# Attention of a fused attention and two-layer network kernel in blocks of 64 keys: one transpose takes two blocks, and the values of a pair go to two PSUM banks

## The chip, the cores and the metric

The kernel runs on one core of a Trainium2 chip. The metric is device time of one launch in microseconds (us). Three runs of the kernel before gave 847.7, 848.0 and 848.58; their median is 848.0.

## The reference

```
scores = q @ k.T / sqrt(64)                    # 4 batches, 8 heads, 576 tokens, 64 wide
heads 0-3: query t sees keys t-31 .. t         # local
heads 4-7: query t sees keys t, t-32, t-64, .. # strided
attn = softmax(scores);  x = attn @ v          # 2304 tokens x 512
g = s * relu(x @ w_in)**2 + b;  y = g @ w_out  # 512 -> 2048 -> 512
h = y @ w2_in;  out = (h * cos(h)) @ w2_out
```

## The kernel before, in words

The two layers take most of the time: 128x512 (or 128x384) fp32r matmuls whose operands are split into a high and a low part, so that each product is three matmuls. They are called big matmuls below. Attention is cut into 20 pairs of heads, five for each batch: two of local heads ("loc"), two of strided heads ("str", queries and keys sorted by token modulo 32, so that a residue is a block of 18 by 18) and one with what the blocks left over of all four ("rem"). Pairs are numbered from 0, so pair 10 is the first of batch 2. `j` is the head of a pair; its 64 channels lie on partitions 64j to 64j+63.

For each pair (class `Item`, one for each head): scores into one PSUM bank for each head (`pair_scores`, tile `s_ps`, L616); maximum, and before it the mask, on VectorE (`mask_max`; for batches 0 and 1 the mask is instead added by a matmul with the identity, L611); exponentials on ScalarE, one instruction for each block with its row sums (`exps`, L548); division by the sums on VectorE (`norm`, L561 to L563); transposes of the blocks on TensorE into `t_ps` (L573); a move out of PSUM on ScalarE (`tevac`, L581); the value matmuls into `o_ps` (L651); and a split of `o_ps` into `xhi` on ScalarE (L143) and `xlo` on VectorE (L146). A loc head has four 128x96 score blocks, each of two groups of 64 queries that see 96 keys; a str head has four of 126x126 (7 residues); a rem head one of 128x96 and two of 72x72.

Two stages run attention. Until batch 0 is done, pairs follow each other alone, with `FILL` dummy bf16 matmuls of 384 columns after the scores of pairs 1 to 5, and with weights of the first layer converted on VectorE between them. Then `attention()` is called between the big matmuls of the first layer's slots, and `Attention.micro` takes one step at a call: values of the pair two back, scores of the newest, then transposes of the one between. Each engine runs its list in the order in which the recording layer put it there; that order is fixed when the program is built, and the layer reorders what `micro` asks for by its own estimate. PSUM has eight banks: four tagged `acc`, three `att`, one `h`. In the second stage scores, transposes and values take turns on the three `att` banks. The probabilities of a head, and what the transposes gave, lie in six buffers (`NPB`).

Masks are made on GpSimd (POOL) at the start (L878 to L888). The loads of batch 0 (`FIRST`) stand in one list on the SP queue.

Of the kernel before, what the change touches and what calls it, by code (L numbers as in the profile page):

```python
# [20 lines left out]
P = 128  # L21
# [7 lines left out]
LG, LK = 64, 96  # L29
SG = 7 * NJ  # L30
SR = S - 4 * SG
# [19 lines left out]
NPB = 6  # L51
# [19 lines left out]
PRE = 3  # L71
WARM = 13
FILL = {1: 6, 2: 5, 3: 5, 4: 5, 5: 5}
# [37 lines left out]
def net(ctx, tc, qkl, qks, rqk, vloc, vstr, rv, wi1, wo1, wp1, wo2, wp2, s, b, out):  # L111
# [22 lines left out]
    mloc = const.tile([P, 4, LK], BF16, name="mloc")  # L134
    mstr = const.tile([SG, SG], BF16, name="mstr")
# [302 lines left out]
    def load_qk(bb, hp):  # L438
        if bb == 0 and hp >= 2:
            t = part[0][hp - 2][:, : QKW * 2].rearrange("p (t c) -> p t c", t=2)  # L440
        else:
            t = io_p.tile([P, 2, QKW], F32, tag="io", name="qk")
        src, w = (qkl, QKW) if hp < 2 else (qks, 4 * SG)
        nc.sync.dma_start(out=t[:, :, :w], in_=src[bb, hp % 2])
        qk_t[bb, hp] = t

    def load_v(bb, hp):
        if bb == 0 and hp >= 2:
            o = (hp - 2) * 4 * P
            v = part[1][0][:, o : o + 4 * P].rearrange("p (n d) -> p n d", d=P)  # L450
        else:
            v = io_p.tile([P, 8, P], F32, tag="v", name="v")
        if hp < 2:
            nc.sync.dma_start(out=v[0:LK], in_=vloc[bb, hp])
        else:
            nc.sync.dma_start(out=v[0:SG, 0:4, :], in_=vstr[bb, hp - 2])
        v_t[bb, hp] = v

    def load_rem_qk(bb):
        r = rem_p.tile([P, 4 * (LK + SR)], F32, tag="rq", name="rq")  # L460
        nc.sync.dma_start(out=r, in_=rqk[bb])
        rem_t[bb] = [
            r[:, : 4 * LK].rearrange("p (h t c) -> p h t c", h=2, t=2),
            r[:, 4 * LK :].rearrange("p (h t c) -> p h t c", h=2, t=2),
        ]

    def load_rem_v(bb):
        t = rem_p.tile([LK, 4, P], F32, tag="rv", name="rv")
# [5 lines left out]
    class Item:  # L474


        def __init__(self, bb, hp, j, kind):
            self.bb, self.hp, self.j, self.kind = bb, hp, j, kind
            self.ready = self.moved = self.stored = False
            if kind == "loc":  # L480
                self.parts = [(P, LK, 4, 0, mloc)]
            elif kind == "str":
                self.parts = [(SG, SG, 4, 0, mstr.unsqueeze(1).to_broadcast([SG, 4, SG]))]
            else:
                self.parts = [
                    (P, LK, 1, 0, mloc[:, 1:2, :]),
                    (SR, SR, 2, LK, mstr[:SR, :SR].unsqueeze(1).to_broadcast([SR, 2, SR])),
                ]
            self.tcols = []
            o = 0  # L490
            for m, k, n, _, _ in self.parts:
                self.tcols.append(o)
                o += m * n

        def score_mms(self):

            r = slice(self.j * D, (self.j + 1) * D)
            if self.kind == "rem":
                rq = rem_t[self.bb][0]
                yield 0, [(LG * hp, 0, rq[r, hp, 0, 0:LG], rq[r, hp, 1, :]) for hp in range(2)]  # L500
                res = []
                for hp in range(2):
                    rs = rem_t[self.bb][1]
                    res.append((0, LK + hp * SR, rs[r, hp, 0, :], rs[r, hp, 1, :]))
                yield 1, res
                return
            t = qk_t[self.bb, self.hp]
            res = []
            for i in range(4):
                if self.kind == "loc":  # L510
                    for g in range(2):
                        o = (2 * i + g) * LG
                        res.append((g * LG, i * LK, t[r, 0, o : o + LG], t[r, 1, o : o + LK]))
                else:
                    o = i * SG
                    res.append((0, i * SG, t[r, 0, o : o + SG], t[r, 1, o : o + SG]))
            yield 0, res

        def view(self, t, i):
            m, k, n, c, _ = self.parts[i]  # L520
            return t[:m, c : c + n * k].rearrange("p (n k) -> p n k", k=k)

        def mask_max(self, alloc):
            self.p = alloc()
            self.sm = sm_p.tile([P, 3, 4], F32, tag="sm", name="sm")
            for i, (m, k, n, c, mask) in enumerate(self.parts):
                src = self.view(self.s_ps, i)
                if not self.pe_mask:
                    dst = self.view(self.p, i)
                    nc.vector.tensor_tensor(dst, src, mask, ALU.add)  # L530
                    src = dst
                nc.vector.tensor_reduce(self.sm[:m, 0, i : i + n], src, axis=AX.X, op=ALU.max, negate=True)  # L532
                nc.vector.tensor_scalar(self.sm[:m, 0, i : i + n], self.sm[:m, 0, i : i + n], SCALE, None, ALU.mult)

        def run_transp(self, tag, alloc):
            self.moved = False
            self.transp(tag)
            yield
            with tc.high_priority():
                self.tevac(alloc, nc.scalar)  # L540
            self.moved = True

        def exps(self):
            for i, (m, k, n, c, _) in enumerate(self.parts):
                dst = self.view(self.p, i)
                src = self.view(self.s_ps, i) if self.pe_mask else dst
                for t in range(n):
                    nc.scalar.activation(  # L548
                        dst[:, t, :],
                        src[:, t, :],  # L550
                        AF.Exp,
                        bias=self.sm[:m, 0, i + t : i + t + 1],
                        scale=SCALE,
                        accum_out=self.sm[:m, 1, i + t : i + t + 1],
                    )

        def norm(self):
            for i, (m, k, n, c, _) in enumerate(self.parts):
                dst = self.view(self.p, i)
                sm = self.sm[:m, :, i : i + n]  # L560
                nc.vector.tensor_scalar_add(sm[:, 1, :], sm[:, 1, :], 1e-9)  # L561
                nc.vector.reciprocal(sm[:, 2, :], sm[:, 1, :])
                normed[0] = nc.vector.tensor_tensor(  # L563
                    dst, dst, sm[:, 2, :].unsqueeze(2).to_broadcast([m, n, k]), ALU.mult
                )

        def transp(self, tag):
            self.t_ps = psum(tag, "t_ps")
            for i, (m, k, n, c, _) in enumerate(self.parts):
                src = self.view(self.p, i)  # L570
                for t in range(n):
                    o = self.tcols[i] + t * m
                    self.moves = nc.tensor.transpose(self.t_ps[:k, o : o + m], src[:, t, :], ident[:m, :m])  # L573

        def tevac(self, alloc, eng):
            self.pt = alloc()
            for i, (m, k, n, c, _) in enumerate(self.parts):
                o = self.tcols[i]
                dst, src = self.pt[:k, o : o + n * m], self.t_ps[:k, o : o + n * m]
                if eng is nc.scalar:  # L580
                    nc.scalar.activation(dst, src, AF.Copy)  # L581
                else:
                    eng.tensor_copy(dst, src)

        def pv_mms(self, o):

            dst = o[self.j * D : (self.j + 1) * D]
            dc = slice(self.j * D, (self.j + 1) * D)
            if self.kind == "rem":
                vr = rem_t[self.bb][2]  # L590
                res = []
                for hp in range(4):
                    m, k, c = (LG, LK, hp * LG) if hp < 2 else (SR, SR, P + (hp - 2) * SR)
                    res.append((dst[:, c : c + m], vr[:k, hp, dc], self.pt[:k, c : c + m]))
                return res
            v = v_t[self.bb, self.hp]
            m, k, n = (LG, LK, 8) if self.kind == "loc" else (SG, SG, 4)
            return [
                (dst[:, i * m : (i + 1) * m], v[:k, i, dc], self.pt[:k, i * m : (i + 1) * m]) for i in range(n)
            ]  # L600

    def pair_scores(pair, tag, pe_mask):

        for it in pair:
            it.s_ps = psum(tag, "s_ps")
            it.pe_mask = pe_mask
        for parts in zip(*[it.score_mms() for it in pair]):
            if pe_mask:
                for it, (pi, _) in zip(pair, parts):
                    m, _, _, _, mask = it.parts[pi]  # L610
                    nc.tensor.matmul(  # L611
# [926 lines left out]
```

## Time and profile before

| what | value |
|---|---|
| median of three runs | 848.0 us |
| span of the profiled execution (the page gives no other time of it) | 845.1 us |
| runs less span | 2.9 us |
| PE busy, share of the span | 835.9 us, 99% |
| DVE busy | 620.4 us, 73% |
| ACT busy | 560.5 us, 66% |
| granted TensorE clock | 1.000 |

A busy PE is one with a matmul between its start and its modelled end; matmuls overlap in that sense, so the time that an instruction costs is read from its start to the start of the next one. "PEld" are the weight loads. An fp32 matmul shows as two matmuls and two weight loads, so 16 in the program are x32 in a row. A form such as "64*126 64x126" names the weights (64 partitions, 126 columns) and then the moving operand.

### The profile page before, as it was taken

What the parts mean: (1) busy time and instruction counts of PE and PEld (TensorE: products, weight loads), DVE (VectorE), ACT (ScalarE), POOL (GpSimd) and SP (SyncE); (2) the same over time, 40 slices, a digit from 0 to 9 for tenths busy, and PEclk for the clock granted to TensorE, in tenths of its full rate; (3) what the DMA queues carried; (4) which work ended last, traced back from release to release, by engine and by line L of the source; (5) the groups of instructions that cost most, each with busy time, mean ns of one, the idle gap of its engine ahead of it and who ended that gap; (6) DMA issues with size and microseconds to landing.
All of it is one profiled execution on the core that took longest, in us unless ns stands there. A gap on an engine that the chain in (4) does not pass through costs nothing.

```text
span 845.1 us, 13962 instructions
## 1 busy us (share of the span) xinstructions
PE 835.9 (99%) x5023; PEld 730.9 (86%) x5023; DVE 620.4 (73%) x1248; ACT 560.5 (66%) x1164; POOL 4.0 (0%) x15
## 2 busy tenths in 40 slices
PE   9999999999999999999999999999999999999998
PEld 6677788889888999999998988988989989889886
DVE  6999988798888779997975896664665555644553
ACT  6898978577777776876776665554754554645543
POOL 1000000000000000000000000000000000000000
PEclk9999999999999999999999999999999999999999
DMA  9855352687788997986899988655755655745412
GB/s 279 266 184 175 117 156 62 207 276 213 253 304 305 342 335 248 291 296 234 304 329 297 296 276 249 216 172 175 254 201 184 211 169 184 278 163 202 158 50 76
DMA packets 73445, 189.90 MB, mean 225 GB/s; under 512 B 7344, under 2 KB 26160, under 8 KB 73376
## 3 DMA queue, kind: packets, MB, share of 16 engines
q1 hardware_dynamic: 72080, 182.58, 65.1%
q10 hardware_dynamic: 1296, 6.42, 2.0%
q8 instruction: 40, 0.66, 0.3%
q14 instruction: 29, 0.24, 0.1%
HBM read 146.51 MB, written 42.47 MB: 224 GB/s over the span
## 4 chain that ended last, share of the span: by engine, by line
PE 88%; DVE 5%; ACT 3%; DMA 2%; issue 1%; POOL 0%; POOLq 0%; DVEq 0%; ACTq 0%
PE acc L1316 21%; PE pa L1422 14%; PE pb L1422 14%; PE acc L790 12%; PE h_ps L790 11%; PE acc L1326 11%; PE o_ps L651 2%; PE t_ps L573 1%; PE s_ps L616 1%; DMA w2s<-ow 1%; DVE xlo L146 1%; DMA wfb<-xlo 1%; ACT part L548 1%; DVE sm L532 0%; DVE gl L146 0%
## 5 line engine op out<-in xcount | busy, mean ns | idle before, releaser
L1316 PE MATMUL acc<-w2l,gh 128*128 128x512 f32 x576 | 177.9, 390 | 0.0
L1422 PE MATMUL pa<-xhi,wfl 128*128 128x384 f32 x464 | 138.2, 338 | 1.5 <-DVE h L1403 1.5
L1422 PE MATMUL pb<-xhi,wfl 128*128 128x384 f32 x464 | 137.9, 337 | 0.0
L1316 PEld LDWEIGHTS acc<-w2l,gh 128*128 128x128 f32 x576 | 107.8, 188 | 21.5
L1316 PE MATMUL acc<-w2l,gl 128*128 128x512 f32 x288 | 112.5, 391 | 0.0
L1232 ACT ACTIVATE r<-h 128x768 f32<-128x768 f32 (+1 forms) x50 | 40.8, 817 | 94.9 <-DVE h L1403 94.6
L146 DVE TENSOR_TENSOR gl<-r,gh 128x768 fp32r<-128x768 f32 (+3 forms) x90 | 71.5, 796 | 42.2 <-ACT gh L1232 39.0
L790 PE MATMUL h_ps<-xhi,w 128*128 128x512 f32 (+1 forms) x320 | 99.7, 375 | 1.4 <-ACT r L813 1.0
L790 PE MATMUL acc<-gh,w 128*128 128x512 f32 (+1 forms) x320 | 98.8, 373 | 0.4 <-ACT gh L143 0.4
L1422 PEld LDWEIGHTS pa<-xhi,wfl 128*128 128x128 f32 x464 | 85.5, 188 | 5.5 <-DVE h L1403 2.5
L1422 PEld LDWEIGHTS pb<-xhi,wfl 128*128 128x128 f32 x464 | 85.5, 188 | 3.1 <-ACT q L1433 0.4
L1326 PE MATMUL acc<-gh,w2l 128*128 128x512 f32 (+1 forms) x384 | 85.2, 336 | 0.0
L1422 PE MATMUL pa<-xlo,wfl 128*128 128x384 f32 x232 | 77.8, 335 | 0.0
L1422 PE MATMUL pb<-xlo,wfl 128*128 128x384 f32 x232 | 77.8, 335 | 0.0
L1403 DVE TENSOR_TENSOR h<-pb,q 128x384 f32<-128x384 f32 x72 | 39.9, 554 | 49.1 <-PE pb L1422 45.2
L790 PEld LDWEIGHTS h_ps<-xhi,w 128*128 128x128 f32 x320 | 58.6, 189 | 12.9 <-ACT r L813 2.2
L790 PEld LDWEIGHTS acc<-gh,w 128*128 128x128 f32 x320 | 58.3, 189 | 11.3 <-ACT gh L143 0.8
L1326 PEld LDWEIGHTS acc<-gh,w2l 128*128 128x128 f32 x384 | 59.8, 188 | 7.2
L1403 DVE TENSOR_TENSOR h<-pa,q 128x384 f32<-128x384 f32 x72 | 39.9, 554 | 33.2 <-PE pa L1422 32.5
L1316 PEld LDWEIGHTS acc<-w2l,gl 128*128 128x128 f32 x288 | 54.0, 188 | 11.3
L1263 ACT ACTIVATE r<-r 128x768 f32<-128x768 f32 (+1 forms) x50 | 40.9, 820 | 33.0 <-DVE r L1261 33.0
L1265 DVE TENSOR_TENSOR r<-h,r 128x768 f32<-128x768 f32 (+1 forms) x50 | 46.1, 925 | 18.8 <-ACT r L1263 18.4
(148 smaller groups left out, 1569.1 us busy)
## 6 DMA issues: line engine op xcount, KB each, us to landing
wfl<-wfb SPq DMA_DIRECT2D x68, 512.0 KB, 4.9
w2l<-w2s SPq DMA_DIRECT2D x60, 512.0 KB, 3.5
wfl<-wfa SPq DMA_DIRECT2D x34, 512.0 KB, 4.2
praw<-in_wp_dram SPq DMA_DIRECT2D x22, 512.0 KB, 4.9
oraw<-in_wo_dram SPq DMA_DIRECT2D x22, 512.0 KB, 4.6
wfb<-ob SPq DMA_DIRECT2D x21, 512.0 KB, 4.2
w2s<-ow SPq DMA_DIRECT2D x20, 512.0 KB, 4.2
wfl<-wfc SPq DMA_DIRECT2D x34, 256.0 KB, 4.7
```

Of the source, the lines that this page charges most:

```text
L146: return nc.vector.tensor_tensor(dst_lo, src, hi.bitcast(F32), ALU.subtract)
L548: nc.scalar.activation(dst[:, t, :], src[:, t, :], AF.Exp, bias=self.sm[:m, 0, i + t : i + t + 1], scale=SCALE, accum_out=self.sm[:m, 1, i ...
L573: self.moves = nc.tensor.transpose(self.t_ps[:k, o : o + m], src[:, t, :], ident[:m, :m])
L651: tail[0] = nc.tensor.matmul(dst, vs, pt, start=True, stop=True)
L790: nc.tensor.matmul(*args, **kw)
L1232: return nc.scalar.activation(*args, **kw)
L1263: nc.scalar.activation(r, r, AF.Sin, scale=-TWO_PI)
L1265: nc.vector.tensor_tensor(r, h[:, a:b], r, ALU.mult)
L1316: nc.tensor.matmul(accs[e], g[:, e * P : (e + 1) * P], w[:, wi, :], start=start and i == 0, stop=stop and i == 2, skip_group_check=True,)
L1326: nc.tensor.matmul(o, w[:, wi, e * P : (e + 1) * P], g[:, c : c + o.shape[1]], start=start and i == 0 and (c == 0 or e % 2 == 0), stop=sto ...
L1403: added[u] = nc.vector.tensor_tensor(hs[f][:, HALVES[half]], bank, qs[q], ALU.add)
L1422: nc.tensor.matmul(pb[bi], a, b[:, m, :], start=st and m == 0 and i == 0, stop=m == 1 and i == 2, skip_group_check=True)
```

## The change

All blocks are 64 keys wide. A loc head has groups of 32 queries (`LG` 64 to 32), four to a 128-row block, each with its 64 keys. A str block has three residues (54 rows and keys, computed 64 wide), two to a 128-row block, so that `SG` is 54 and not 126; 24 of the 32 residues are in the str pairs, and the rem pair takes eight (144 tokens) where it took four. Each head now has four 128x64 blocks in every pair (class `Pair`, in place of two `Item`). One transpose takes two blocks (128x128), a pair's four transposes fill one bank, and one 128x512 move takes all of it. After it the keys of one block lie on partitions 0 to 63 and of the other on 64 to 127, so the value matmuls use 64 rows and 64 columns of the array each, and the two row halves write two banks, `o[0]` and `o[1]`, each split to `xhi` and `xlo` apart. In the second stage a step takes the transposes of a pair, the scores of the next, and then the values of the same pair. `NPB` goes from 6 to 4, and the fill is of 256 columns with counts that keep the columns nearly the same. The values of the rem pair move to another buffer; v and rem loads grow, q and k of str pairs shrink.

```
-    def transp(self, tag):                      # per head: one per block
-            for t in range(n):
-                self.moves = nc.tensor.transpose(self.t_ps[:k, o : o + m], src[:, t, :], ident[:m, :m])
+        def transp(self, j, tag):
+            if j == 0:
+                self.t_ps = psum(tag, "t_ps")
+            for u in range(2):
+                src = self.p[:, j, 2 * u : 2 * u + 2, :].rearrange("p n k -> p (n k)")
+                o = 256 * j + P * u
+                self.moves = nc.tensor.transpose(self.t_ps[:, o : o + P], src, ident)
+        def run_move(self, alloc):
+            with tc.high_priority():
+                self.pt = alloc()
+                nc.scalar.activation(self.pt, self.t_ps, AF.Copy)
+        def scores(self, tag, pe_mask, alloc):
+            s_ps = [psum(tag, "s_ps") for _ in range(2)]
...
+            for part, po, lq, lk in self.score_mms():    # loc: 4 parts x 4 groups, str: 4 x 2
+                for j in range(2):
+                    r = slice(j * D, (j + 1) * D)
+                    self.last = nc.tensor.matmul(
+                        self.s[j][po : po + lq.shape[1], part, :], lq[r], lk[r], start=not pe_mask, stop=True, ...
+        def values(self, o):
+            for b_, c, slot_, q, w in self.value_mms():  # b_ alternates 0, 1; w = 32 (loc), 54 (str)
+                r = slice(KT * b_, KT * b_ + KT)
+                for j in range(2):
+                    d = slice(j * D, (j + 1) * D)
+                    tail[0] = nc.tensor.matmul(
+                        o[b_][d, c : c + w], v[r, slot_, d], self.pt[r, 256 * j + q : 256 * j + q + w], start=True, stop=True
+                    )
+        def dests(self, o):                      # two halves, each its own xhi and xlo
...
 def micro(self):
-                if done:
-                    while not (done[0].moved and done[1].moved):
-                        tick()
-                    spawn(run_values(*done, self.tags[2]))
...
+                    while self.valued < q - 1:
+                        self.values()
+                        yield
+                    if old:
+                        yield from self.transposes(old)
+                    if new:
+                        with tc.issue_after(tail[0].ins):
+                            self.scores(new, q)
+                    yield
+                    self.values()
+                    yield
...
-    for g in range(2):
-        m = mloc[g * LG : (g + 1) * LG]
+    for a in range(4):
+        m = mloc[a * LG : (a + 1) * LG]
         for base, km, cm in ((-1, 1, -1), (32, -1, 1)):
             nc.gpsimd.affine_select(
-                out=m, in_=m, ..., pattern=[[0, 4], [km, LK]], channel_multiplier=cm
+                out=m, in_=m, ..., pattern=[[0, 4], [km, KT]], channel_multiplier=cm
...
+    nc.gpsimd.memset(mrem[:, 1:4, :], NEG)       # then 6 memsets and 12 selects of 64x54
...
-NPB = 6
+NPB = 4
-FILL = {1: 6, 2: 5, 3: 5, 4: 5, 5: 5}
+FILL = {1: 9, 2: 8, 3: 8, 4: 8, 5: 8}
```

On PE before, around the values of pair 10 (bank `o_ps_1824`), the last transposes of the pair, twelve big matmuls, and then the values in one run:

```order
L573 MATMUL t_ps_1797<-ident_87,part21_102 96x128 x4
L790 MATMUL h_ps_1802<-xhi_92,w0_345 128x512
L790 MATMUL h_ps_1802<-xlo_93,w0_345 128x512
L790 MATMUL h_ps_1802<-xhi_92,w0_345 128x512 x2
L790 MATMUL h_ps_1802<-xlo_93,w0_345 128x512
L790 MATMUL h_ps_1802<-xhi_92,w0_345 128x512 x2
L790 MATMUL h_ps_1802<-xlo_93,w0_345 128x512
L790 MATMUL h_ps_1802<-xhi_92,w0_345 128x512 x2
L790 MATMUL h_ps_1802<-xlo_93,w0_345 128x512
L790 MATMUL h_ps_1802<-xhi_92,w0_345 128x512
L651 MATMUL o_ps_1824<-part21_102,v_1616 64x64 x16
L616 MATMUL s_ps_1841<-qk_1716 126x126
```

On PE now, the end of the 32 score matmuls of pair 11 (`s_ps_1496`, `s_ps_1497`), which stand right behind the last transposes of pair 10 (`t_ps_1489`), and then the values of pair 10 in its two banks `o_ps_1564` and `o_ps_1565`:

```order
L530 MATMUL s_ps_1496<-qk_1253 32x64
L530 MATMUL s_ps_1497<-qk_1253 32x64
L609 MATMUL o_ps_1564<-part20_101,v_1360 64x32 x16
L786 MATMUL acc_1236<-gh_1348,w1_1190 128x512
L786 MATMUL h_ps_1718<-xhi_92,w0_576 128x512
L609 MATMUL o_ps_1565<-part20_101,v_1360 64x32 x16
L786 MATMUL h_ps_1718<-xlo_93,w0_576 128x512
```

No big matmul is left between a pair's transposes and its values, and the values stand bank by bank, the first 16 on one row half of the array and the other 16 on the other. The values stand so, in two runs, in the ten pairs 6 to 15 (pair 11's without big matmuls between); in pairs 0 to 5 and 16 to 19 the banks alternate.

On ACT before, the moves of pair 10 stand between the exponentials of pair 11 (`sm_1751` is its second head), and the split of pair 10's values follows them:

```order
L548 ACTIVATE part21_102,sm_1751<-part21_102,sm_1751 128x96
L581 ACTIVATE part21_102<-t_ps_1792 96x512
L581 ACTIVATE part21_102<-t_ps_1797 96x512
L548 ACTIVATE part21_102,sm_1751<-part21_102,sm_1751 128x96 x3
L813 ACTIVATE r_1817<-h_ps_1802 128x512
L814 ACTIVATE r_1817<-r_1817 128x512
L143 ACTIVATE xhi_92<-o_ps_1824 128x512
```

On ACT now, the move of pair 10, the two splits of its values, and behind them all exponentials of pair 11:

```order
L809 ACTIVATE r_1615<-h_ps_1598 128x512
L810 ACTIVATE r_1615<-r_1615 128x512
L147 ACTIVATE w1_2891<-wtmp_2892 128x512
L155 ACTIVATE wtmp_2962<-wraw_2957 128x256
L579 ACTIVATE part20_101<-t_ps_1489 128x512
L147 ACTIVATE gh_1664<-r_1615 128x512
L155 ACTIVATE wtmp_2962<-wraw_2959 128x256
L147 ACTIVATE xhi_92<-o_ps_1564 128x256
L147 ACTIVATE xhi_92<-o_ps_1565 128x256
L550 ACTIVATE part20_101,sm_1494<-part20_101,sm_1494 128x64 x4
L550 ACTIVATE part20_101,sm_1495<-part20_101,sm_1495 128x64 x4
```

The exponentials of a pair have moved behind the splits of the pair before it, and so behind the second run of its values.

## Rows read from the trace of the kernel before

**Rows 1.** Windows: length, busy us of PE, PEld, DVE, ACT, POOL, clock, DMA share, GB/s.
```profile
4.00:32.00 28.00, 26.93 (x370) 18.87 (x370) 23.85 (x81) 22.28 (x104) 0.83 (x4) 1.00 1.04 314
...
60.00:100.00 40.00, 38.93 (x377) 30.30 (x374) 37.93 (x123) 35.11 (x126) 0.00 (x0) 1.00 0.53 166
100.00:160.00 60.00, 60.00 (x493) 48.55 (x492) 48.12 (x154) 45.55 (x157) 0.00 (x0) 1.00 0.36 108
```
**Rows 2.** Waits of PEld, 32 to 160 us, largest: total us, times, longest.
```profile
PEld o_ps L651 <- ACT part L581: 2.5, 7, 0.4
```
**Rows 3.** Timeline of PE around three pairs: start, us, what, count.
```profile
61.47 0.59 PE L573 MATMUL t_ps<-ident,part 126*126 126x126 f32 x4
61.82 0.47 PE L790 MATMUL acc<-gh,w 128*128 128x512 f32 x1
...
65.42 1.08 PE L651 MATMUL o_ps<-part,v 126*64 126x126 f32 x16
66.43 0.89 PE L616 MATMUL s_ps<-qk 64*64 64x96 f32 x32
67.25 0.50 PE L790 MATMUL h_ps<-xhi,w 128*128 128x512 f32 x1
67.59 0.39 PE L790 MATMUL h_ps<-xlo,w 128*128 128x512 f32 x1
67.82 0.39 PE L790 MATMUL h_ps<-xhi,w 128*128 128x512 f32 x1
...
70.80 0.70 PE L651 MATMUL o_ps<-part,rv 96*64 96x64 f32 x16
71.43 0.89 PE L616 MATMUL s_ps<-qk 64*64 64x96 f32 x32
...
76.05 1.04 PE L573 MATMUL t_ps<-ident,part 128*96 128x128 f32 x8
76.84 0.48 PE L790 MATMUL h_ps<-xlo,w 128*128 128x512 f32 x1
...
78.07 0.39 PE L790 MATMUL acc<-gh,w 128*128 128x512 f32 x1
78.39 1.15 PE L651 MATMUL o_ps<-part,v 96*64 96x64 f32 x32
79.47 1.15 PE L616 MATMUL s_ps<-qk 64*126 64x126 f32 x16
80.55 0.50 PE L790 MATMUL acc<-gh,w 128*128 128x512 f32 x1
```
**Rows 4.** Timelines of narrow windows: first matmuls and first weight loads of runs.
```profile
66.43 0.29 PE L616 MATMUL s_ps<-qk 64*64 64x96 f32 x1
66.43 0.31 PE L616 MATMUL s_ps<-qk 64*64 64x96 f32 x4
...
13.26 0.14 PEld L651 LDWEIGHTS o_ps<-part,v 96*64 96x64 f32 x2 [0.32 <-ACT part L581]
13.26 0.20 PEld L651 LDWEIGHTS o_ps<-part,v 96*64 96x64 f32 x4 [0.32 <-ACT part L581]
```
**Rows 5.** DVE and ACT groups by form: count, busy us, mean ns, idle before, releaser.
```profile
L563 DVE TENSOR_TENSOR part<-part,sm 126x504 f32<-126x504 f32 x16 | 10.8, 676 | 0.2
L563 DVE TENSOR_TENSOR part<-part,sm 128x384 f32<-128x384 f32 x16 | 8.8, 552 | 0.2
...
L548 ACT ACTIVATE part<-s_ps,sm 128x96 f32<-128x96 f32 x36 | 11.7, 347 | 6.6 <-DVE sm L533 5.6 <-DVE sm L562 1.0
L581 ACT ACTIVATE part<-t_ps 96x512 f32<-96x512 f32 x16 | 8.8, 587 | 1.4 <-PE t_ps L573 1.4
L869 ACT ACTIVATE part<-acc 128x256 f32<-128x256 f32 x4 | 1.3, 376 | 0.2 <-PE acc L790 0.2
```
**Rows 6.** The mask selects on POOL, and PE's first work that needs them.
```profile
L882 POOL TENSOR_SCALAR_AFFINE_SELECT mloc<-mloc 64x384 bf16<-64x384 bf16 x4 | 2.1, 524 | 0.2
...
4.08 0.80 PE L611 MATMUL s_ps<-mloc,identb 128*128 128x384 bf16 x2
```

More of the change, by code (lines that the diff above doesn't have):

```diff
@@ L712, in batch_done, with scores @@
         def batch_done(self, bb):
-            return self.pairs[5 * bb + 4][1].stored
+            return self.pairs[5 * bb + 4].stored
         @property
         def done(self):
-            return self.n > len(self.pairs) + 1
+            return self.valued == len(self.pairs) and self.pairs[-1].stored
+        def scores(self, pair, q):
+            spawn(run_scores(pair, self.tags[0], pair.bb < PE_MASK, self.alloc))
+            tail[0] = pair.last
+            fill(FILL.get(q, 0), pair.last)
@@ L720, in transposes @@
         def transposes(self, pair):
-            for it in pair[::-1] if self.grouped else pair:
-                while not it.ready:
+            for j in range(2):
+                while not pair.ready[j]:
                     tick()
-                with tc.issue_after(tail[0].ins) if self.grouped and it is pair[0] else nullcontext():
-                    spawn(it.run_transp(self.tags[1], self.alloc))
-                tail[0] = it.moves
+                pair.transp(j, self.tags[1])
+                tail[0] = pair.moves
+                if j:
+                    stages.append(pair.run_move(self.alloc))
@@ L727, in transposes, with values @@
                 if not self.grouped:
                     yield
[L729 to L730 removed]
+        def values(self):
+            pair = self.pairs[self.valued]
+            while not pair.moved:
+                tick()
+            self.valued += 1
+            spawn(run_values(pair, self.tags[2]))
         def micro(self):
[L733 removed]
+            while self.valued < len(self.pairs):
                 q = self.n
[L735 to L752 removed]
@@ new lines, in micro @@
+                new, old = self.pair(q), self.pair(q - 1)
+                if not self.grouped:
+                    self.scores(new, q)
+                    yield
+                    if q >= 2:
+                        self.values()
+                        yield
+                    if old:
+                        yield from self.transposes(old)
+                else:
+                    while self.valued < q - 1:
+                        self.values()
+                        yield
+                    if old:
+                        yield from self.transposes(old)
+                    if new:
+                        with tc.issue_after(tail[0].ins):
+                            self.scores(new, q)
@@ L753, in micro @@
                     yield
-                if old:
-                    yield from self.transposes(old)
+                    self.values()
+                    yield
                 bb, k = divmod(q, 5)
@@ L919, in net @@
                 bg_step(EARLY_BG)
[L920 to L921 removed]
+        if early < 2 and att.pairs[PRE // 2 + early].stored:
             mm_h(0, early)
```

381 lines of the change are left out of this document (168 added, 213 removed).

## The prediction

> **What bounds the kernel now.** I read the windows by stage first, then the waits of PE, then PE's timeline around three pairs, and last the groups by form. The windows [rows 1] have one line for each stage; the reader is to see who is full. From 60 to 100 us PE is busy 38.93 of 40 us, DVE 37.93, ACT 35.11; from 100 to 160 us PE is busy all the time and DVE and ACT have a fifth to a quarter free. So from batch 1 on PE sets the time, with DVE and ACT close behind. In batch 0 (4 to 32 us) PE is busy 26.93 of 28 us only because dummy matmuls fill it; DVE has 23.85 and ACT 22.28 us of work there in chains through all three engines, and DMA is at its full share (1.04, 314 GB/s). The clock is 1.00 in each stage. The largest wait of PE's weight loads for ACT's moves comes to 2.5 us in 7 waits, none over 0.4 us [rows 2]: the two-step distance between a pair's transposes and its values hides the move. So a microsecond less of attention on PE after batch 0 is a microsecond of the end, if no wait comes in its place, and attention before 32 us counts by its chain instead.
>
> The cost of a run of small matmuls is its start to the next run's start [rows 3]: loc scores 67.25 - 66.43 = 0.82, str values 66.43 - 65.42 = 1.01, loc values 79.47 - 78.39 = 1.08, str scores 80.55 - 79.47 = 1.08, rem values 71.43 - 70.80 = 0.63, eight transposes 76.84 - 76.05 = 0.79, four 61.82 - 61.47 = 0.35. A big matmul costs 67.82 - 67.59 = 0.23; the one ahead of a run costs 78.39 - 78.07 = 0.32 and the one behind 67.59 - 67.25 = 0.34, so another run between big matmuls adds about 0.2.
>
> **A model of the small runs.** The first four score passes end 0.31 after their start and the first alone 0.29 [rows 4]: passes on different quarters start within 20 ns of each other. I call one pass on each free part of the array a round. Loc scores are 8 rounds of 96 columns, str values 8 of 126 (two halves), loc values 16 of 64 (two halves). Three costs give three unknowns: 8(126 - 96)a = 1.01 - 0.82, a = 0.79 ns a column; then 7 ns a round and 0.15 us a run. A round of 64 columns is 0.058 us. The second pair of 64-column weight loads ends 0.06 later than the first [rows 4], the same figure, so a round of 64 weight columns and 32 moving ones is between 0.032 (moving columns set it) and 0.058 (loads set it); I take 0.058, since the loads show it.
>
> **The change, part by part, on PE.** All in us; 8 loc, 8 str and 4 rem pairs.
> - Scores: loc 64 passes of 64 columns on 32-column parts, eight together, so 8 rounds: 0.46 + 0.15 = 0.62, -0.2. Str 32 passes on four quarters, also 0.62, -0.46. Rem I count as even. Sum -5.3. No row shows eight together; with four it is 16 rounds, 1.08.
> - Transposes: four a pair, 0.35. Loc -0.44, str -0.35 (two heads of 0.35 before), rem about -0.1: -6.8.
> - Values with all four quarters: loc 64 passes, 16 rounds, 1.08, even; str 8 rounds 0.62, -0.39; rem 12 rounds 0.85, +0.22: -2.2. If moving columns set the rounds, loc is 0.66.
> - Masks by matmul (20 of them): 128 columns less at 0.23 / 512 a column: -1.1.
> - Against that, the instruction order: in pairs 6 to 15 the two banks are not alternated. The 16 matmuls of one bank stand before the 16 of the other, and one row half of the array has two quarters, so each run needs as many rounds as all four quarters would for both. Loc pairs 6, 10 and 15 gain 1.08 + 0.2, pair 11 some 0.7; str 7, 8, 12, 13 gain 0.62 + 0.2 each; rem 9 and 14 0.8: +9.5.
>
> PE's work is thus -15.4 + 9.5 = -5.9. Of the -15.4, batch 0 has 2 x 0.64 + 2 x 1.2 + 0.5 for masks, about -4.1, which the dummies stand in for. Outside batch 0: **-1.8**.
>
> **Waits.** The old 2.5 us go for the most part, since the values no longer stand where they stood: **-1.0**. In the new order scores of the next pair (0.62) and hardly a big matmul stand between the transposes and the values. The last transposes end 0.59 - 0.35 = 0.24 after the next run could start [rows 3], the move takes 0.59 [rows 5], and ACT is in the middle of something of about 0.6, half of it on average: 0.24 + 0.3 + 0.59 - 0.62 = 0.5, a little less where a big matmul stands between. Nine steps (pairs 7 to 15) at 0.45: **+4.0**. Behind the waiting values stand the big matmuls, and DVE and ACT wait for those. With nothing ahead on ACT it is 0.2 each, 1.9 in all; with two such instructions ahead about 1.1 and 9 or so.
>
> **Batch 0.** One move instead of two (-0.59), two splits of 0.376 for one of 0.588 (+0.16), and eight exponentials of 64 columns, 0.03 shorter each: ACT has 0.7 less in a loc pair. DVE's four wide operations of a pair go from 552 or 676 ns to about 420 (the two rows give 1.03 ns a column), -0.5 or -1.0, with 0.15 more for the second xlo [rows 5]. Five pairs: ACT and DVE lose some 2.5 to 3 us each of a chain that both stand in; I take -3.0 (bounds 0 and -5). The masks: eight selects on POOL for four of 524 ns, and PE's first scores stand at 4.08 us right behind them [rows 6]. Eight selects cost 2.8 us (by columns) to 4.2 (no shorter), so the start is 0.7 to 2.1 later; PE's first pair then runs against the same loads, and I take +0.7. Loads of batch 0 grow by 445 KB by their shapes, at 314 GB/s 1.4 us; only the rem pair, last of the five, needs the grown ones late: +0.3. Batch 0: **-2.0** (bounds -4.5 and +3.5).
>
> **Sum:** -2.0 - 1.8 - 1.0 + 4.0 = -0.8, I say -1. The profiled execution had a span of 845.1; 844.1 now. The runs shown lie 2.9 above the span (848.0), which I keep: **847.0 us**.
>
> [...]
>
> **Rivals.**
> - *Rounds go by moving columns, and waits are hidden.* Then loc values are 0.43 a run shorter: three pairs with two runs save 2.6, pairs 11 and 16 some 1.0, rem 0.5, and waits are 2 instead of 4: -6, **841**. For it: matmul costs here follow columns. Against: the load row. Chance 0.24.
> - *Values, splits and exponentials become a loop.* On ACT all exponentials of pair q+1 now stand behind both splits of pair q, so behind the second run of values. Once round: transposes and their end 0.6, move 0.6, two runs 2 x 1.28, splits 0.75, eight exponentials 8 x 0.31 = 2.5, normalisation of 0.42 and small operations 0.4: 7.8 us. Values of successive pairs stood at 65.42, 70.80 and 78.39 [rows 3], steps of 5.4 and 7.6 us. It decides wherever the step is under the loop, which DVE and ACT at 95% and 88% can't shorten; 1.2 us in five of pairs 9 to 15 is +6: **853**. Against: big matmuls can be drawn in between, and pairs with less work have a shorter loop. Chance 0.20.
> - *Only four passes together in loc scores.* +0.47 in six pairs outside batch 0: **850**. Against: the parts are independent in the rows seen. Chance 0.08.
> - *PE can't start passes faster than its densest run so far*, 0.82 / 32 = 0.026 us each. Loc scores would be 64 x 0.026 = 1.64, +1.0 in six pairs; str scores 0.82, +0.2 in six; alternated values +0.9 together; batch 0 +2: **857**. Against: the four starts within 20 ns [rows 4]. Chance 0.06.
>
> [...]
>
> **How the numbers follow.** The forecast has 0.42 (own range 843.5 to 850). A measurement of this kernel can tell 0.2%, 1.7 us, from no change: same is 846.3 to 849.7. Of the 0.42, 0.16 are faster, 0.21 same, 0.05 slower. The first rival adds 0.24 to faster; the other three add 0.34 to slower. Faster 0.40, same 0.21, slower 0.39. The range is 840 to 855: below it lies the far end of the first rival, above it the last and part of the loop, together under 0.2.
>
> **What would show it.** Right: loc score runs of about 0.62 and 32 matmuls of 32 columns (64 passes) in runs of 1.1 for one bank; waits of the values for ACT's move of 0.2 to 0.7 in pairs 7 to 15; batch 0 ending some 2 us sooner. Wrong: two-run loc values near 1.3 in all (first rival), PE idle over 1 us a pair before exponentials' products (loop), score runs of 1.1 or 1.6 (the last two), or first scores later than 6 us.

## The result, and the profile after

The changed kernel took 855.73 us (median of 4 runs, 854.42 to 856.88), 1.0094 times the kernel before (95% interval 1.0079 to 1.0108); timed again it was 855.27 us, 1.0083 times (1.0062 to 1.0104). The forecast was 847.0 with a range of 840 to 855: it is slower, and just outside. The profiled execution had a span of 852.6 us, 7.5 more than before.

The windows of the changed kernel, first by the stages of [rows 1] with 32 to 60 us added, columns as there:

```profile
4.00:32.00 28.00, 23.64 (x590) 17.53 (x588) 19.78 (x75) 19.70 (x104) 5.52 (x24) 0.94 0.97 358
32.00:60.00 28.00, 26.00 (x378) 19.91 (x379) 23.83 (x71) 21.45 (x80) 0.00 (x0) 0.88 0.53 167
60.00:100.00 40.00, 39.83 (x573) 31.59 (x572) 35.54 (x112) 33.78 (x119) 0.00 (x0) 0.96 0.54 165
100.00:160.00 60.00, 59.01 (x793) 45.98 (x793) 41.04 (x136) 42.57 (x167) 0.00 (x0) 1.00 0.37 118
```

The second stretch in the kernel before:

```profile
32.00:60.00 28.00, 27.21 (x230) 20.53 (x226) 27.60 (x75) 25.37 (x87) 0.00 (x0) 1.00 0.57 189
```

What differs from before is the column that was 1.00 in every line: the granted clock is 0.94, 0.88 and 0.96 in the first three. DVE and ACT have less to do, as worked out, and from 60 us on PE is busy all the same. Narrower windows of the same kernel, in pairs: what stood ahead of each fall of the clock, and the fall:

```profile
17.75:19.30 1.55, 0.00 (x0) 0.00 (x0) 1.55 (x7) 1.24 (x5) 0.00 (x0) 1.00 1.02 410
19.50:22.90 3.40, 3.40 (x42) 2.44 (x42) 2.41 (x10) 2.01 (x9) 0.00 (x0) 0.50 0.91 269
40.10:41.85 1.75, 0.00 (x0) 0.00 (x0) 1.75 (x6) 1.75 (x5) 0.00 (x0) 1.00 0.55 139
43.40:50.15 6.75, 6.75 (x57) 4.90 (x51) 4.69 (x14) 3.99 (x16) 0.00 (x0) 0.50 0.38 127
79.90:84.35 4.45, 4.41 (x135) 3.59 (x135) 3.86 (x10) 2.76 (x7) 0.00 (x0) 1.00 0.66 197
84.40:87.80 3.40, 3.40 (x10) 2.62 (x9) 2.73 (x11) 2.78 (x17) 0.00 (x0) 0.50 0.57 182
```

Three times the granted clock was 0.50 instead of 1.00, for 3.4, 6.75 and 3.4 us. In the third fall a big matmul took 0.43 us from start to start (84.99 to 85.42), behind it 0.23 (87.89 to 88.12). Counted as half of the time at 0.50, an estimate, the three are a loss of 6.8 us of PE work, where the span grew by 7.5. Counted in both timelines, the 400th big matmul, which stands behind attention, comes at 174.81 us and before at 169.45: 5.4 of the 7.5 us arise ahead of it. Less the 6.82 that the falls lost, it would stand at 167.99, 1.5 sooner than before. Ahead of the first two falls PE had stood idle for 1.61 and 1.87 us; ahead of the third it had a matmul under way for 4.41 of 4.45 us, but mostly small ones: the scores of pair 11 and both runs of values of pair 10, these on two quarters of the array each (64*64, one row half). PE's timeline in the changed kernel (start, us, what, count):

```profile
5.45 0.58 PE L526 MATMUL s_ps<-mloc,identb 128*128 128x256 bf16 x2 [1.43 <-POOL mloc L882]
...
16.94 0.78 PE L609 MATMUL o_ps<-part,v 64*64 64x32 f32 x39
19.33 0.82 PE L609 MATMUL o_ps<-part,v 64*64 64x32 f32 x25 [1.61 <-issue]
...
37.78 1.14 PE L609 MATMUL o_ps<-part,v 64*64 64x32 f32 x64
38.84 0.50 PE L786 MATMUL h_ps<-xhi,w 128*128 128x512 f32 x1
39.19 0.39 PE L786 MATMUL h_ps<-xlo,w 128*128 128x512 f32 x1
39.42 0.38 PE L574 MATMUL t_ps<-ident,part 128*128 128x128 f32 x2
39.55 0.48 PE L786 MATMUL h_ps<-xhi,w 128*128 128x512 f32 x1
41.91 0.50 PE L786 MATMUL acc<-gh,w 128*128 128x512 f32 x1 [1.87 <-ACT gh L147]
...
55.05 0.69 PE L530 MATMUL s_ps<-qk 64*64 64x64 f32 x32
55.66 0.67 PE L609 MATMUL o_ps<-part,v 64*64 64x54 f32 x16
56.26 0.50 PE L786 MATMUL acc<-gh,w 128*128 128x512 f32 x1
...
81.14 1.12 PE L609 MATMUL o_ps<-part,v 64*64 64x32 f32 x32
82.20 0.50 PE L786 MATMUL acc<-gh,w 128*128 128x512 f32 x1
...
113.98 0.86 PE L530 MATMUL s_ps<-qk 64*32 64x64 f32 x64
114.77 0.89 PE L609 MATMUL o_ps<-part,part 64*64 64x32 f32 x24
```

The sizes, by starts as in [rows 3]: all 64 value passes of a loc pair with alternating banks 38.84 - 37.78 = 1.06, and 32 of them on one bank also 82.20 - 81.14 = 1.06 (1.08 forecast for each); str values of one bank 0.60 (0.62 for a run); str scores 0.61 (0.62); two transposes 0.13, so 0.27 for a pair (0.35); loc scores 0.79 (0.62). The first idle stretch cuts a run of values in two, and PE waited there for nothing that the profile shows ("issue"). The second is a wait of a big matmul for `gh`, which ACT makes between the pieces of attention.

PEld's waits of the changed kernel, 32 to 160 us (total us, times, longest), against [rows 2]:

```profile
PEld acc L786 <- ACT gh L147: 2.2, 1, 2.2
PEld s_ps L530 <- issue: 2.0, 6, 1.0
PEld o_ps L609 <- ACT part L579: 1.5, 5, 0.5
```

The wait that I priced at 4.0 us, of the values for the move, comes to 1.5. The idle time of PE itself from 32 to 160 us, whatever ended it, is 3.9 us, before 1.9.

### The profile page after: what moved, and what is told of

Its sections match the earlier page's. It is cut to its first block, busy times and chain, and to the rows that moved or that the text cites. A ratio compares the mean times of both kernels' runs of the same rounds, so it can differ in the third digit from the quotient of the medians.

```text
span 852.6 us, 15772 instructions
## 1 busy us (share of the span) xinstructions
PE 837.6 (98%) x5922; PEld 732.2 (86%) x5922; DVE 608.3 (71%) x1220; ACT 553.8 (65%) x1168; POOL 8.6 (1%) x36
## 4 chain that ended last, share of the span: by engine, by line
PE 86%; DMA 4%; DVE 4%; ACT 4%; issue 1%; POOL 0%; POOLq 0%; ACTq 0%; DVEq 0%
PE acc L1316 21%; PE pa L1422 13%; PE pb L1422 13%; PE h_ps L786 12%; PE acc L786 10%; PE acc L1326 10%; PE o_ps L609 3%; DMA w2s<-ow 2%; PE s_ps L530 2%; PE t_ps L574 1%; DVE gl L150 1%; DVE xlo L150 1%; DMA wfb<-xlo 1%; DMA praw<-in_wp_dram 1%; ACT part L550 1%
## 5 line engine op out<-in xcount | busy, mean ns | idle before, releaser
L786 PE MATMUL h_ps<-xhi,w 128*128 128x512 f32 (+1 forms) x320 | 104.9, 389 | 0.0
L786 PE MATMUL h_ps<-xlo,w 128*128 128x512 f32 (+1 forms) x160 | 60.7, 380 | 0.0
```

The lines of the kernel that those rows point to most:

```text
L786: nc.tensor.matmul(*args, **kw)
```

## The experiments

Three theories of the lost 7.5 us stood against each other: the falls of the clock (the clock theory: half of 3.4, 6.75 and 3.4 us is lost); the PE work of the values in two runs (the two-run theory); and the loop of the forecast's rival over ACT and DVE (the loop theory). "Loss" below is the share of a run below full clock times its span; "span" is always the device's own, some 1.8 us under the time.

**Dummies ahead of two falls.** In `transp`, behind the first two transposes of pair 6, and ahead of the scores of pair 11:

```
+HOLD_T = {(1, 1): 8}          # (batch, pair of heads): dummies of 128x256 into the other half of t_ps
+HOLD_S = {(2, 1): 6}          # into s_ps, ahead of the scores
```

The dummies have 14 x 256 columns, at 0.23 us for 512 some 1.6 us of PE. By the clock theory the two later falls go, half of 6.75 and 3.4 us, and the time is 855.7 - 5.1 + 1.6 = 852.2.

> The changed kernel with 14 more dummy matmuls of 256 columns (8 behind the first two transposes of pair 6, ahead of the stretch in which PE idles at 40 to 42 us; 6 ahead of the scores of pair 11, near 80 us), nothing left out. [...] Rival (PE work of the values in two runs): the clock is a symptom, 856 to 858 with the dummies' 1.6 us on top. Rival (loop over ACT and DVE): 856, the dummies fill waits and the clock makes no difference.

Measured 848.89 us, 1.0021 times before (1.0006 to 1.0037), 7 us less than the changed kernel with 14 matmuls more, and 3 less than even the 852.2 of the clock theory. Its windows, then the place of the second fall in its timeline:

```profile
20.00:32.00 12.00, 10.21 (x227) 7.57 (x234) 9.12 (x34) 8.32 (x43) 0.00 (x0) 0.86 0.79 303
32.00:60.00 28.00, 27.14 (x420) 20.65 (x408) 25.81 (x79) 24.67 (x91) 0.00 (x0) 1.00 0.60 194
60.00:100.00 40.00, 39.73 (x596) 31.63 (x595) 37.06 (x117) 34.43 (x127) 0.00 (x0) 1.00 0.57 172
```
```profile
40.12 1.04 PE L544 MATMUL t_ps<-mloc,identb 128*128 128x256 bf16 x8
40.92 0.48 PE L795 MATMUL h_ps<-xhi,w 128*128 128x512 f32 x1
42.04 0.97 PE L795 MATMUL acc<-gh,w 128*128 128x512 f32 x3 [0.65 <-ACT gh L149]
```

`gh` is no sooner (42.04 against 41.91), but the idle time ahead of it is 0.65 and the clock stays at 1.00 from 32 us on; one fall is left ahead of that, from 28.14 to 31.55 us. The dummies also moved some later instructions (pair 10's two runs of values now stand one right behind the other, 64 passes in 2.27 us), so two controls were run.

**The same dummies elsewhere** (`HOLD_T = {(2, 3): 8}`, `HOLD_S = {(3, 1): 6}`).

> Control of the run with 14 dummies: the changed kernel with the same 14 dummy matmuls at other places, 8 behind the first transposes of pair 13 and 6 ahead of the scores of pair 16 (near 105 and 125 us, where the clock did not fall). Clock theory: the falls at 19.5, 43 and 84 us stay as they are, 855 to 857. Rival (the 14 dummies helped by moving the order of the instructions): some 849, as with the dummies at pairs 6 and 11.

Measured 852.93 us, 1.008 times (1.0048 to 1.0111). Its windows:

```profile
20.00:32.00 12.00, 9.68 (x295) 7.20 (x295) 9.94 (x39) 9.74 (x52) 0.00 (x0) 1.00 0.82 305
32.00:60.00 28.00, 26.14 (x325) 19.90 (x321) 23.87 (x71) 21.52 (x78) 0.00 (x0) 0.88 0.55 180
60.00:100.00 40.00, 39.85 (x593) 31.67 (x592) 36.91 (x116) 33.52 (x116) 0.00 (x0) 1.00 0.58 174
```

The fall behind 42 us is there as in the changed kernel; those at 19.5 and 84 us were absent in this execution, though nothing was done about them. It lies between both theories: 4 us above the dummies at the right places, 2 us under what I expected.

**The 8 dummies at pair 6 alone** (`HOLD_S = {}`).

> The changed kernel with the 8 dummies behind the first two transposes of pair 6 alone (no dummies at pair 11). Clock theory: the fall at 43 us (one or two stretches of 3.4 us, 1.7 to 3.4 us lost) goes, that at 84 us stays (1.7): 850 to 851, and span less the loss 845 to 846. Rival (the gain of the 14 dummies came from the changed order around pairs 10 and 11): 854 to 856.

Measured 851.87 us, 1.0052 times (1.004 to 1.0064). No fall behind 42 us in its trace, none at 84 us either. Span less loss is 845.3 to 849.2 over its 5 runs, above what the clock theory said in four of them: some 1 to 2 us of it are not the clock's. A fall from 28.43 to 31.85 us is left in this trace too.

**The same order, other falls.** Two kernels leave PE's order as it is and move the time at which things stand. One has 32 tiny matmuls more while PE waits for the masks, the other makes the local mask on 64 columns and copies it:

```
+    for _ in range(32):
+        nc.tensor.matmul(dummy[:, :16], warm[:, :P], warm[:, :16], start=True, stop=True, ...)
```
```
-        m = mloc[a * LG : (a + 1) * LG]                      # selects over 4 x 64 columns
+        m = mloc[a * LG : (a + 1) * LG, 0, :]                # over 64
+    nc.gpsimd.tensor_copy(mloc[:, 1:4, :], mloc[:, 0:1, :].to_broadcast([P, 3, KT]))
```

> The changed kernel with the local mask made on 64 columns and copied to the other 192: PE's first scores would start about 0.8 us earlier (4.6 for 5.45 us), the order on PE is the same. If the start of batch 0 counts for the end: -0.8, 855. If loads or instruction supply decide batch 0: no change, 855 to 856. Clock theory: a moved start also moves where the falls of the clock stand against the work; if a fall goes, -1.7, if one is added, +1.7.

> The changed kernel with 32 tiny matmuls of 16 columns more before the first scores, while PE waits for the masks anyway; the order of all else is the same. Instruction-supply theory: PE's pauses in which it waited for nothing that the profile shows stand at its instructions 706, 962 and 1218, 256 apart, in all kernels with the new blocks; they stay at these numbers and so fall 64 instructions (matmuls and weight loads) earlier in the program, the first before or in the values where it now stands at their 40th matmul. Rival (these pauses belong to a place in the program, a semaphore that the profile doesn't show): they stay at the same matmul of the program. Time 853 to 858 by either.

> The kernel with 32 tiny matmuls more before the first scores, timed more often: the order of all other instructions is that of the changed kernel, but the pauses for instructions stand elsewhere, and so the falls of the clock. Clock theory: span less the time lost to the clock (share below full clock times span) is 845 to 846.5 as in the changed kernel (845.7), and a run at clock 0.999 or 1.000 takes a span of 845 to 847. Rival (half of the loss is in the order itself, as the slope of 0.44 over the ten runs of the changed kernel would have it): 849 to 850 at clock 1.000.

> The changed kernel itself, unaltered, timed more often, for the granted clock of each run beside its span. Clock theory: where the falls stand differs from run to run, since the same program's runs of before lie within 1%; over the runs the span grows by 1 us for each us lost to the clock (share below full clock times span), and the line meets zero loss at 845 to 846, the span of the kernel before; the median lies at 852 to 856. Rival (waits and two-run values cost the time): spans don't follow the clock, and a run at clock 1.000 still takes 852.

The mask kernel missed its aim: selects of the other mask came between the narrow ones and the copy, and PE's first scores started at 6.68 us, not 4.6. It took 850.78 us (1.0052 times, 1.0027 to 1.0078) all the same. Over its ten runs the granted clock went from 0.990 to 1.000 and the span from 854.8 to 845.3, slope 1.01 +- 0.11 us for each us of loss; its two runs at 1.000 had spans of 845.3 and 846.0. The kernel with tiny matmuls took 851.36 us (one run) and 853.2 us (six, 1.0062 times, 1.0037 to 1.0086); its run at 1.000 had a span of 846.6, its run at 0.991 one of 853.0. The changed kernel never ran at full clock: ten runs, 0.987 to 0.998, mean loss 7.9 us, spans 850.5 to 855.1; by itself its slope is 0.44 +- 0.08. All 27 runs of this one order together: slope 0.82 +- 0.07, span 847.0 +- 0.4 at no loss, where the kernel before has a median span of 845.7. So of the 8 us, 0.82 x 7.9 = 6.5 go with the clock, and 1 to 2 don't. This is an estimate: by the changed kernel's own slope only 3.5 would go with it, by the mask kernel's all 7.9, and why its own slope is lower is open.

The traces say the same without a slope. In the five traces of this order the 400th big matmul stands at 171.7 to 177.8 us; less half of each fall ahead of it, at 167.55 to 169.99, where the kernel before has 169.45. The idle time ahead of `gh` is in all five (1.85 to 1.88 us). Four have a fall behind it; in a second trace of the changed kernel it lasts longest:

```profile
43.70:57.30 13.60, 13.44 (x116) 10.23 (x117) 7.59 (x21) 7.74 (x27) 0.00 (x0) 0.50 0.37 113
```

In the mask kernel's trace the same idle time stands ahead of `gh`, and the clock stays at 1.00 (its timeline, then its window):

```profile
43.83 0.50 PE L786 MATMUL acc<-gh,w 128*128 128x512 f32 x1 [1.86 <-ACT gh L147]
```
```profile
32.00:60.00 28.00, 25.62 (x409) 19.31 (x410) 26.81 (x81) 24.76 (x97) 0.00 (x0) 1.00 0.64 205
```

**Values in one run, same step order.** Each value matmul is queued behind the one before it (issue order only):

```
+                    with tc.issue_after(prev.ins) if prev else nullcontext():
+                        prev = tail[0] = nc.tensor.matmul(o[b_][d, c : c + w], ...)
```

> The changed kernel with the value matmuls of a pair held in their alternating order of banks (issue order only), so that they stand in one run on four quarters but for the first two of them. Two-run theory: loc pairs fall from 2.2 to about 1.3 us of PE, str from 1.2 to 0.8, ten pairs, some -6 to -7 us: 849. Clock theory: of the three falls only the one at 84 us hung on the thin stretch of values in two runs; the idle at 17.7 and at 40 us stays: -2 to -3, 853. Loop theory: the values come later, behind the read-out of the next pair's first score bank, so exponentials too: 856 to 860.

Measured 849.06 us, 1.0018 times (0.9996 to 1.004), clocks from 0.989 to 0.999; span less loss averages 843.1, against 845.7 for the changed kernel. The two-run theory's figure, but only 2.6 us of it at equal clock.

**Step order of before** (values of the pair two back, scores, transposes), banks not held:

> The changed kernel (its blocks, banks, moves, fills) with the step order of the kernel before in the second stage: values of the pair two back, scores of the newest, transposes of the one between. Values alternate the banks in most pairs, but the scores of a pair stand in two runs, one for each head (about +0.6 us a pair). Loop theory: the waits between transposes, values and exponentials go, -4 to -6: 850. Two-run theory: what the values get back (-7) the scores give up (+8): 856. Clock theory: the time follows what the clock does; with less idle of PE at 40 us no fall there, 850 to 852.

Measured 849.9 us, 1.0028 times (1.0013 to 1.0042), span less loss 844.5: the time that the clock theory gave, but the loop theory gave 850 as well, so this run does not tell the two apart; against a loop stands that PE was busy for 98.8 of the 100 us from 60 to 160 in the changed kernel. At equal clock it is 1.2 us less than the changed kernel: values that stand in one run in most pairs, against scores that stand in two.

**Values ahead of the scores** in a step:

> The changed kernel with the values of a pair ahead of the scores of the next in a step (transposes, values, scores), in the second stage. The values alternate the banks in all pairs with four big matmuls ahead of them; the scores stand in two runs, one for each head, with 1 to 5 big matmuls between. Two-run theory: -9 for the values, +8 for the scores: 855. Loop theory: values no longer wait behind the next scores, and the splits of a pair end before the exponentials of the next are ready: 850. [...]

Measured 857.55 us, 1.0125 times (1.0082 to 1.0167), span less loss 850.9. No theory said this much; why this order is 5 us worse at equal clock I did not follow up.

**Dummies of 512 columns** (5, 4, 4, 4, 4 of them in place of 9, 8, 8, 8, 8), nothing else:

> The changed kernel with dummies of 512 columns (5, 4, 4, 4, 4) in place of 256 (9, 8, 8, 8, 8): 20 matmuls and 20 weight loads less in batch 0. Instruction supply: PE's pauses stay at its instructions 706, 962 and 1218, which now stand 10 to 40 instructions further on in the program; batch 0 a little sooner. Two-run values and idle at 40 us stay: 851 to 856 by the clock theory, by what the falls do. If the dummies made the gain of the combined run: 844.

Measured 848.91 us, 1.0009 times (0.9996 to 1.0022): clocks of 0.996 to 0.999 and spans of 845.4 to 848.5. The order around 40 us came out otherwise, with an idle stretch of 0.49 in place of 1.87 us, and the clock did not fall behind it. That is neither expected figure, 851 to 856 or 844: the three falls of the changed kernel are absent from its trace, one from 28.98 to 32.39 us stands there instead, and nothing in the edit aimed at that.

**Both one-run edits with the step order of before:**

> The new blocks with the step order of the kernel before in the second stage, and the values and scores of a pair held in alternation of banks and heads, so that each stands in one run but for a first matmul or two; masks and dummies as in the changed kernel. If the gain of the combined run (842 us) came from the order: 842 to 844. If from its 512-column dummies: 847 to 849.

Measured 844.54 us, 0.9966 times (0.9946 to 0.9986): the order made the gain. Its trace has idle time of 1.57 us up to 19.91 us, and no fall behind it or in the rest of attention. Its windows and a pair of its timeline:

```profile
32.00:60.00 28.00, 27.53 (x426) 19.82 (x422) 27.57 (x85) 24.69 (x98) 0.00 (x0) 1.00 0.67 219
60.00:100.00 40.00, 39.88 (x662) 29.90 (x660) 38.40 (x130) 35.28 (x133) 0.00 (x0) 1.00 0.60 184
```
```profile
94.77 0.69 PE L613 MATMUL o_ps<-part,v 64*64 64x54 f32 x32
95.38 0.30 PE L532 MATMUL s_ps<-qk 64*32 64x64 f32 x2
95.61 0.50 PE L790 MATMUL h_ps<-xhi,w 128*128 128x512 f32 x1
...
97.09 0.84 PE L532 MATMUL s_ps<-qk 64*32 64x64 f32 x62
```

Values of a str pair now stand in one run of 0.61 us, and scores in one but for their first. Over 12 runs its spans are 839.5 to 848.8, 840.3 on average less the loss.

**With 512-column dummies and the narrow mask as well**, first as in the mask run, then with the local mask's selects kept ahead (`tc.high_priority()`):

> The changed kernel's blocks with the step order of the kernel before in the second stage, score and value matmuls held in alternation (one run each but for a first matmul or two), the mask of the run above, and dummies of 512 columns in place of 256 (half as many instructions, the same columns within 12%). Clock and waits: no stretch with two-run values, two-step distance between transposes and values, so no fall after 32 us: before -1.8 of PE work -2 of batch 0, 844 to 846. Rival (the pauses for instructions and the fall that follows stay in batch 0): 847 to 848. Rival (two-run theory alone): 849.

> The combined run again (step order of before, one run of values and of scores, 512-column dummies), with the local mask's selects of 64 columns kept ahead of those of the other mask, so that PE's first scores start at about 4.9 us and not at 6.7. Batch 0 starts 1.8 us sooner than in the combined run: if its chain sets the start of the second stage, 841.5; if loads or instruction supply do, 843.

Measured 842.99 us (0.9961 times, 0.9944 to 0.9977), and 844.18 us (0.9945 times, 0.9925 to 0.9965). Both beat the kernel before and the changed one. The second started its scores at 5.07 us instead of 6.68 and was not clearly better, since the intervals overlap: 1.6 us at batch 0's start do not show at the end.

## Why the prediction was wrong

The step that failed stands in the prediction's first paragraph: "The clock is 1.00 in each stage" was read off the kernel before and carried into the kernel after. No term of the sum and no rival had the clock in it. It is worth about 6.5 us over the 27 runs of this order (3.5 to 7.9 by which slope one takes), and 6.8 us of PE work in the trace. The rest by its steps:

- **PE's work** was nearly right where runs are small: values 1.06 for 1.08, str scores 0.61 for 0.62, transposes even 0.08 less. A round of values with 32 moving columns is (1.06 - 0.15) / 16 = 0.057 us, with the forecast's 0.15 for a run: the figure taken from the loads, and the first rival (0.032) falls. Loc scores were 0.17 too cheap: 64 passes in 0.79 us, 12 ns each, so more than four parts run together (four would be 1.08, a pass each 0.026 us would be 1.64), but eight do not cost what four cost. Why is open. That is 1.0 us in six pairs.
- **Values in two runs** stood as read from the order, and each run cost what both would. What it was worth at equal clock, 2.6 us for the step order of the change, is less than the 9.5 that I counted. My reading, argued from the order and not tested by itself, is that the run that replaces it has to wait for its second bank: in that kernel's trace four value passes of pair 6 stand at 46.81 us and the other 60 at 49.74. With the two-step order, and the scores held in one run as well, span less loss goes from 845.7 to 840.3.
- **Waits**: +4.0 forecast for values behind the move, 1.5 found. In their place came one of 1.9 us for `gh` that I did not see: ACT had the pieces of attention ahead of it. As a wait it is 1.9 us at most; the fall behind it lost 3.4. In all, PE's idle time from 32 to 160 us grew by 2.0, where the two terms for waits came to +3.0.
- **Batch 0**: PE's first big matmul stands at 20.41 us, before at about 22.0 (counted in both timelines), -1.6 for -2.0, though the masks cost +1.4 at the start (5.45 against 4.08 in [rows 6]), in the middle of their bounds, and PE stood idle for 1.61 us ahead of 19.33 us.
- **The loop** did not come: PE is busy 98.8 of the 100 us from 60 to 160.

The sum without the clock, 844.1, compares with 845.7 to 847.0 of span at no loss: right in kind, 2 to 3 us short. That the total lands this near is in part luck: the scores were 1.0 too cheap and the waits 1.0 too dear.

What sets the clock off is open; for one of the three falls the runs show with what it went. With 8 dummies in the idle stretch ahead of it (0.65 us idle in the first such kernel, 1.87 without them), the fall behind 42 us was absent in both kernels that had them, and present where they stood elsewhere. Over all 16 traces: where the idle time of 1.85 to 1.88 us stood ahead of `gh`, the fall came in seven of eight (the mask kernel's is the exception); in the other eight, where it was 0.65 at most, in none. For the first fall the traces only agree: in the 15 traces with the new blocks 22 falls begin between 8 and 160 us, and 21 of them begin in or right behind idle time of PE of 1.2 to 3.7 us, the pauses described at the end or the wait for `gh`. But 15 idle stretches of 1.1 to 2.2 us had no fall behind them, so what decides is open. The kernel before has idle stretches of 0.64 us at most there and no fall. The third fall, behind the thin stretch ahead of 84 us, is not explained: the same stretch stands in the other four traces of this order, one of them of the changed kernel itself, and none has a fall there.

The 2 us that the two profiled executions differ by after attention (the 400th big matmul stands 5.4 us later, the end 7.5) lie within the spread of the traces, and so are no shown cost of the new blocks: from that matmul to the end it is 677.8 us in the changed kernel and 675.7 before, and in the other traces with the new blocks 675.1 to 677.7, one of 683.0 aside (values ahead of the scores), which has a further fall there.

## What to carry to other kernels

In this case faster small matmuls left PE with idle stretches (3.9 us from 32 to 160 us, before 1.9), and the granted clock of the kernel before (1.000 in its trace) did not speak for the kernel after (0.992): for every stretch in which a change takes work from PE, ask what fills it, and look at the granted clock of each run before explaining a loss by instructions. Where a run needs two PSUM banks at once, count the banks that the stage has: here three for five uses a step, and it was the order, of the steps and within a pair, that decided whether both halves of the array worked at once (64 value passes in 1.06 us with alternating banks, 32 in 1.06 on one). Before giving up a change that lost, change its order: the same blocks were 0.9% slower or, by order alone, 0.3% faster.

## What the runs showed that I had not expected

**PE's pauses, 256 instructions apart.** In each of the kernels with the new blocks PE paused ahead of its 706th instruction, and mostly ahead of the 962nd or the 1218th, 256 apart, whatever stood there. Counted are matmuls, weight loads, and what PE's sequencer does for semaphores and a drain (7 of these ahead of the 706th). In the changed kernel's trace the pauses are 1.61 us ahead of the 706th and 0.83 ahead of the 1218th, up to 19.33 and 32.13 us. Its page has a queue of instruction loads (packets, MB, share):

```profile
q8 instruction: 47, 0.77, 0.3%
```

That is 16 KB a packet. The page does not name the engine, but PE's trace has 12055 instructions, 47 times 256 and 23 more; the kernel before has 40 of these packets, and its PE 10251 instructions, 40 times 256 and 11 more. So I count 256 instructions to a packet, 64 bytes each, an estimate from these numbers. A window from 0 into the pause counts what PE has started; of the changed kernel, then of the one with 32 tiny matmuls more (two pauses):

```profile
0.00:18.50 18.50, 15.22 (x349) 11.05 (x349) 9.96 (x41) 11.26 (x56) 8.62 (x36) 1.00 0.91 347
```
```profile
0.00:18.00 18.00, 15.79 (x349) 11.65 (x349) 9.34 (x39) 10.57 (x55) 8.38 (x36) 1.00 0.91 344
0.00:24.50 24.50, 20.49 (x476) 15.33 (x476) 15.46 (x58) 14.65 (x74) 8.38 (x36) 1.00 0.88 331
```

And where the latter's pauses stand in its timeline:

```profile
17.12 0.31 PE L609 MATMUL o_ps<-part,v 64*64 64x32 f32 x7
18.30 1.06 PE L609 MATMUL o_ps<-part,v 64*64 64x32 f32 x57 [0.87 <-issue]
...
22.56 0.44 PE L609 MATMUL o_ps<-part,part 64*64 64x54 f32 x13
25.63 0.55 PE L609 MATMUL o_ps<-part,part 64*64 64x54 f32 x19 [2.63 <-issue]
```

Both pause after 349 matmuls and 349 weight loads; in one that is the 40th matmul of a run of values, in the other, with 64 instructions more ahead of it, the 8th of the same run. So the place is one of the instruction stream, not of the work. The traces also hold the time of each packet of that queue. In all 15 kernels' traces with the new blocks each of these pauses ends 1.2 to 1.5 us after one of its packets: in the changed kernel the packet ends at 17.91 us and PE goes on at 19.33, in the one with 32 tiny matmuls more packets end at 16.91 and 24.30 and PE goes on at 18.30 and 25.63. In the kernel before, the packet ahead of the 706th instruction ends at 25.93 us, 5.0 us before PE comes to it, and there is no pause. My reading, which no run tests by itself, is that PE waits there for that load, and that pieces that run faster reach the place before it. The pauses are 0.8 to 2.6 us in these two kernels, with a DMA share of 0.88 to 0.91 in the windows above, and up to 3.7 us (8 dummies at pair 6). What such a pause costs by itself was not tried; all 14 falls of the clock that begin between 8 and 37 us in these traces begin in or right behind one.

**One program, many times.** The mask kernel's ten runs spread over 9.6 us (847.05 to 856.61), the kernel before over 5.3 in 27 runs: where the granted clock differs from run to run, one execution says little, and the medians of two kernels with the same order (855.73 and 850.78) can lie 5 us apart.
